# Where three sets of transposes are made in a two-layer training step: backward weights, feed-forward inputs and normalised queries

## The chip, the cores and the metric

The kernel runs on one core of a Trainium2 chip. The core has a matrix engine (TensorE, PE in the profile, with PEld for its weight loads), a vector engine (VectorE, DVE), an activation engine (ScalarE, ACT), a general engine (GpSimd, POOL) and a queueing engine (SyncE, SP), which here issues nearly all DMAs. Each engine works through its own instructions in their order; semaphores hold an instruction until what it needs is there. Sixteen DMA engines move the data. The metric is the device time of one execution in microseconds; less is better.

## What is computed

Four residual blocks in a row, and all gradients. Block A is attention without softmax over 32 heads of 16; block B is a gated feed-forward. Both share their weights between their two uses. Sequence 2048, width 512, feed-forward width 1376, bf16.

```python
def _A_ref(x, wqkv, wo):
    qkv = (x @ wqkv).reshape(B, S, 3, H, Dh).transpose(2, 0, 3, 1, 4)
    q, k, v = qkv[0], qkv[1], qkv[2]
    phi = lambda t: jnp.where(t > 0, t + 1, jnp.exp(t)) + 1e-6
    pq, pk = phi(q), phi(k)
    kv = jnp.einsum("bhsd,bhse->bhde", pk, v)
    z = jnp.einsum("bhsd->bhd", pk)
    num = jnp.einsum("bhqd,bhde->bhqe", pq, kv)
    den = jnp.einsum("bhqd,bhd->bhq", pq, z)[..., None] + 1e-6
    return (num / den).transpose(0, 2, 1, 3).reshape(B, S, D) @ wo

def _B_ref(x, w_gate, w_up, w_down):
    g = jnp.einsum("bsd,df->bsf", x, w_gate)
    u = jnp.einsum("bsd,df->bsf", x, w_up)
    return jnp.einsum("bsf,fd->bsd", _sigmoid(g) * u, w_down)

x = x + _A_ref(_layernorm(x), wqkv, wo)
x = x + _B_ref(_layernorm(x), w_gate, w_up, w_down)
x = x + _A_ref(_layernorm(x), wqkv, wo)
x = x + _B_ref(_layernorm(x), w_gate, w_up, w_down)
_out, _vjp = jax.vjp(_f, x, wqkv, wo, w_gate, w_up, w_down)
```

The outputs are the result, the gradient of x and the five weight gradients.

## The kernel before

The sequence is cut into 16 tiles of 128 rows (`st` 0 to 15). The blocks are numbered 0 to 3: 0 and 2 are attention, 1 and 3 feed-forward. In time the kernel runs these stages:

- `kq_fwd(0)`: keys, queries and the per-head products of block 0.
- `ab_fwd(0, 1)`, the *lower pass*, about 70 to 204 us: one loop over the tiles does the rest of block 0's attention and all of block 1.
- `kq_fwd(2)` and `ab_fwd(2, 3)`, the *upper pass*, about 261 to 396 us, the same for blocks 2 and 3.
- `b_bwd_p1(3)`, `a_bwd_p1(2)`, `b_bwd_p1(1)`, `a_bwd_p1(0)`: the backward stages. The products for the weight gradients (object `W`) are put between their steps and run alone for some stretches.

Order: within `manual_schedule(engines=EM)` PE, ACT, DVE and POOL take their instructions in the order in which the program writes them. SP's order is made by a planner; `tc.issue_after(ins)` holds the DMAs written in its block behind `ins` on SP's queue.

One step `st` of the two forward passes works on three tiles at once. For most steps (2 to 14, those in `HH_DMA`) the program writes:

1. POOL: a small fill of `hh_t` (L982) and `A.prod(st + 3)`, the product of queries and key sums (L840).
2. PE: `gu` for the first third of the feed-forward width (L922: four matmuls each for gate and up), with ACT's two sigmoids (L924, L926), DVE's product `hh_t` (L929) and POOL's `ssd_t` (L930).
3. `attn_y(st + 2)`: four matmuls from the transposed queries `pqnT` (L884), DVE's add (L892) and the statistics for the layer norm (DVE; POOL L452 to L455, the last making `ln_nmr`).
4. `front1(st + 3)`, `front2(st + 3)`: on DVE the row sums of `prod` (L846), their reciprocals and the normalised queries `pqnstage` (L863). After each odd tile the pair is stored to HBM (L867).
5. `finish` of an earlier tile: eleven matmuls with `wd` (L956) and DVE's add (L958). Step 3 has none.
6. the second and third `gu`; between them `ln.stage_T(st + 1)`: PE transposes the normalised input of the next tile in four blocks into PSUM (L374, `ln_tp<-ident,hstage`), and ACT copies it to the SBUF tile `hT` (L383).
7. `ln.apply(st + 2)` on ACT: the normalised input of the tile after that, `hstage` (L460).
8. `front3(st + 3)`: PE transposes `pqnstage` in four blocks (L374), ACT copies it to `pqnT`.
9. SP: `dma_T`, the DMA transpose of `hh_t` (L949), then the stores of `ssd_t` (L1051), `hh_t` to `sv_hdd` (L1052) and to `sv_hdl` (L1054), and then what `side[st]` holds, behind the last store.

The backward pass of the feed-forward needs the three weights transposed: `wdT`, `wuT`, `wgT`. In the lower pass `wT_units` makes them once: nine units, each a DMA transpose of up to 512x512 from the weight in HBM to a staging tile `wt_st` (L404, L406, L420) and a store to HBM scratch (L409, L412, L421), two of them ahead of the pass and one behind every second step. `b_weight_loads` (L198) then loads the scratch copies with plain DMAs, twice: behind steps 2, 5 and 8 of the upper pass for `b_bwd_p1(3)`, and before `b_bwd_p1(1)`. The last block of the width has 96 rows, and each matmul on it (L1250) uses 96.

In `b_bwd_p1`, `transposes` (L1198) transposes thirds of `dd` on PE, and ACT copies them to `ddT`; in the last third the full blocks (L1209) and the 96-row block (L1211) are copied apart.

## Time and profile before

| | us |
|---|---|
| median of 3 timed runs | 1138.35 (1138.16 to 1139.49) |
| the profiled execution | 1136.78 |
| its span, first to last instruction | 1135.1 |
| granted TensorE clock, mean | 0.998 of full |

Largest groups of PE, from the list of costliest groups (busy time over the whole span; the matmuls' times overlap, so that a group's time in the queue is read from one start to the next):

| line | what | instructions | busy us |
|---|---|---|---|
| L1509 | weight gradients from `p_set`, `p_a` | 2032 | 210.1 |
| L922 | gate and up | 750 | 177.4 |
| L1250 | `dh_ps` in the feed-forward's backward pass | 687 | 164.8 |
| L956 | feed-forward's last product | 340 | 80.6 |
| L374 | `ln_tp`, transposed inputs | 128 | 12.6 |
| L374 | `t_ps` and `ln_tp`, transposed queries | 120 | 11.7 |

The DMA queue that SP issues on moved 280.03 MB and was busy for 88.8% of sixteen engines' span. In a timeline the columns are start, duration (us), engine, line, operation, tiles, shapes and count; square brackets hold the engine's idle time before it and what ended it. In a table by stretch they are the stretch, its length, busy time of PE, PEld, DVE, ACT and POOL with counts, the granted clock, the DMA engines' busy share (packets overlap, so it can exceed 1) and GB/s.

### The profile page before, as it was taken

The numbers are of one execution on the slowest core, as the hardware profiler recorded it, in microseconds if no ns is written. First come the engines' busy times: TensorE is split into PE (matmuls) and PEld (weight loads), VectorE is DVE, ScalarE is ACT, GpSimd is POOL, SyncE is SP. The second block draws the span as 40 slices with busy tenths as digits, with TensorE's granted clock in tenths as the row PEclk, the third lists the DMA queues.
The fourth block names the chain that finished last, engine by engine and source line by source line (L and its number), as shares of the span: only waits on it lengthen the run. The fifth ranks groups of instructions, "written<-read, shape, count | busy, mean of one in ns | idle before, by whom it ended". The sixth has DMA issues, their size and how long they took to land. (4 is left out here: it accounts for less than half of the span.)

```text
span 1135.1 us, 19895 instructions
## 1 busy us (share of the span) xinstructions
PE 1104.4 (97%) x7358; PEld 649.9 (57%) x7468; DVE 696.4 (61%) x1344; ACT 484.6 (43%) x909; POOL 293.8 (26%) x518
## 2 busy tenths in 40 slices
PE   8989999997999999999999999999999999999998
PEld 4444554444545555554446468855556745448888
DVE  6787876777667466665975850166664976851221
ACT  6666666555665633332625431234324515410000
POOL 5647776435666400000110220000000110210000
PEclk9999999999999999999999999999999999999999
DMA  8967999855899999997999897799898899979996
GB/s 268 310 197 210 283 272 273 252 145 174 228 262 282 267 265 257 317 249 191 248 281 278 218 253 239 199 280 288 249 284 257 211 278 290 222 213 299 258 209 191
DMA packets 413682, 282.36 MB, mean 249 GB/s; under 512 B 198608, under 2 KB 399504, under 8 KB 409744
## 3 DMA queue, kind: packets, MB, share of 16 engines
q1 hardware_dynamic: 412432, 280.03, 88.8%
q8 instruction: 58, 0.95, 0.3%
q10 hardware_dynamic: 1152, 1.05, 0.3%
q14 instruction: 40, 0.33, 0.1%
HBM read 125.44 MB, written 115.70 MB: 212 GB/s over the span
## 5 line engine op out<-in xcount | busy, mean ns | idle before, releaser
L1509 PE MATMUL p_ps<-p_set,p_a 128*128 128x256 bf16 (+1 forms) x2032 | 210.1, 264 | 0.1
L1509 PEld LDWEIGHTS <-p_a 128*128 128x128 bf16 x2048 | 185.9, 98 | 22.2
L1130 DVE TENSOR_TENSOR dd<-dhh_ps,ssd 128x512 bf16<-128x512 f32 x144 | 82.4, 628 | 122.7 <-PE dhh_ps L1108 118.9
L1250 PEld LDWEIGHTS <-ddT 128*128 128x128 bf16 (+1 forms) x704 | 67.6, 98 | 74.3 <-DMA ddT<-dd 1.9
L922 PEld LDWEIGHTS <-hT 128*128 128x128 bf16 x768 | 72.8, 98 | 65.3 <-issue 0.8
L930 POOL TENSOR_TENSOR ssd_t<-hh_t,oms 128x512 bf16<-128x512 bf16 (+1 forms) x96 | 100.2, 1054 | 38.2 <-ACT hT L383 16.9
L1082 POOL TENSOR_SCALAR ab<-c 128x2 f32<-128x2 f32 x64 | 12.5, 195 | 375.5 <-DVE junk L1079 358.1
L1209 ACT COPY ddT<-T_ps 128x1024 bf16<-128x1024 bf16 (+1 forms) x72 | 58.8, 819 | 114.7 <-PE T_ps L1207 62.0
L929 DVE TENSOR_TENSOR hh_t<-u_ps,ssd_t 128x512 bf16<-128x512 f32 (+1 forms) x96 | 59.3, 631 | 59.9 <-PE u_ps L922 31.3
L1074 ACT ACTIVATE t_sb<-dh_ps,rstd_all 128x512 f32<-128x512 f32 x64 | 44.0, 688 | 116.0 <-issue 61.7
L924 ACT ACTIVATE ssd_t<-g_ps 128x512 bf16<-128x512 f32 (+1 forms) x96 | 53.4, 556 | 88.8 <-PE g_ps L922 78.7
L922 PE MATMUL u_ps<-wu,hT 128*128 128x512 bf16 (+1 forms) x378 | 89.7, 356 | 0.5
L922 PE MATMUL g_ps<-wg,hT 128*128 128x512 bf16 (+1 forms) x372 | 87.7, 357 | 0.6 <-DVE hT L381 0.2
L1483 DVE TENSOR_TENSOR dw_stg<-p_ps,dw_stg 128x512 bf16<-128x512 f32 (+3 forms) x43 | 28.1, 653 | 98.1 <-PE p_ps L1509 84.2
L1250 PE MATMUL dh_ps<-wgT,ddT 128*128 128x512 bf16 (+1 forms) x343 | 83.9, 379 | 0.4
L1250 PE MATMUL dh_ps<-wuT,ddT 128*128 128x512 bf16 (+1 forms) x344 | 80.9, 379 | 1.0 <-DMA ddT<-dd 0.4
L956 PE MATMUL y_ps<-wd,hhT 128*128 128x512 bf16 (+1 forms) x340 | 80.6, 379 | 1.2 <-DVE x L958 0.6
L1493 PE MATMUL p_ps<-p_a,p_set 128*128 128x512 bf16 (+1 forms) x342 | 80.1, 379 | 0.6
L1108 PE MATMUL dhh_ps<-wdT,gTb 128*128 128x512 bf16 (+1 forms) x323 | 72.5, 356 | 0.6
L956 PEld LDWEIGHTS <-hhT 128*128 128x128 bf16 (+1 forms) x352 | 34.3, 98 | 41.1 <-issue 0.7
L926 ACT ACTIVATE oms<-g_ps 128x512 bf16<-128x512 f32 (+1 forms) x96 | 52.7, 549 | 3.3 <-POOL ssd_t L930 2.4
L1493 PEld LDWEIGHTS <-p_set 128*128 128x128 bf16 (+1 forms) x352 | 33.5, 100 | 34.9
(227 smaller groups left out, 1817.8 us busy)
## 6 DMA issues: line engine op xcount, KB each, us to landing
p_set<-sv_hdd SPq DMA_DIRECT2D x30, 1024.0 KB, 6.1
sv_ssd<-ssd_t SPq DMA_DIRECT2D x32, 688.0 KB, 4.2
ssd<-sv_ssd SPq DMA_DIRECT2D x24, 688.0 KB, 4.9
sv_hdd<-dd SPq DMA_DIRECT2D x24, 512.0 KB, 4.4
sv_hdd<-hh_t SPq DMA_DIRECT2D x32, 320.0 KB, 4.3
p_a<-sv_h SPq DMA_DIRECT2D x16, 512.0 KB, 6.0
p_set<-sv_dqk SPq DMA_DIRECT2D x8, 1024.0 KB, 7.3
h_ld<-sv_h SPq DMA_DIRECT2D x24, 256.0 KB, 4.6
```

Of the source, the lines that this page charges most:

```text
L922: nc.tensor.matmul(ps[:, 0:w], lhsT=hT[:, kc, :], rhs=w_sb[:, kc, c0:c0 + w], start=(kc == 0), stop=(kc == NDC - 1))
L924: nc.scalar.activation(ssd_t[:, 0, c0:c0 + w], g_ps[:, 0:w], ACT.Sigmoid)
L926: nc.scalar.activation(oms[:, 0:w], g_ps[:, 0:w], ACT.Sigmoid, scale=-1.0)
L929: nc.vector.tensor_tensor(hh_t[:, c0:c0 + w], u_ps[:, 0:w], ssd_t[:, 0, c0:c0 + w], ALU.mult)
L930: nc.gpsimd.tensor_tensor(ssd_t[:, 1, c0:c0 + w], hh_t[:, c0:c0 + w], oms[:, 0:w], ALU.mult)
L956: nc.tensor.matmul(y_ps[:], lhsT=T["hhT"][0:r, fc, :], rhs=k.wd[0:r, fc, :], start=(fc == 0), stop=(fc == NFC - 1))
L1108: k.nc.tensor.matmul(ps[:, 0:w], lhsT=gT[:, jc, :], rhs=k.wdT[:, jc, c0:c0 + w], start=(jc == 0), stop=(jc == NDC - 1))
L1130: k.nc.vector.tensor_tensor(dd_part(dd, a, fs), ps[:, 0:w], ssd[:, a, c0:c0 + w], ALU.mult)
L1209: nc.scalar.copy(out[:, :, 0:nfull, :], tps[:, :, 0:nfull, :])
L1250: nc.tensor.matmul(T["dh"][:], lhsT=T["ddT"][0:r, dd_block(a, fc), :], rhs=(k.wuT, k.wgT)[a][0:r, fc, :], start=(i == 0), stop=(i == 2 * N ...
L1493: nc.tensor.matmul(ps[0:r, :], lhsT=set_t[:, st, c * P:c * P + r], rhs=self.ops[j["l"], "g"][:, st, :], start=(st == 0), stop=(st == NST - 1))
L1509: nc.tensor.matmul(ps[:, icl * w:(icl + 1) * w], lhsT=self.ops[j["l"], "h"][:, st, ic * P:(ic + 1) * P], rhs=set_t[:, st, 0:w], start=(st ...
```

## The change

1. The scratch copy of the weights and `wT_units` go. `b_weight_loads` transposes each weight from HBM straight into its SBUF tile, at both places of use, in nine units (three for each weight; the third unit of `wuT` and of `wgT` has two DMAs). In the upper pass two units follow each of steps 0 to 3 and one follows step 4. The last block now takes the last 128 columns, of which the first 32 repeat the block before; a fill on POOL sets those 32 rows to zero after the transpose, and the matmuls use all 128 rows. Accordingly `transposes` in the backward pass takes the last 128 columns of `dd`, with one ACT copy for a third.
2. The feed-forward's inputs of tiles 4 to 15, in both passes, are transposed by a DMA from `hstage` to `hT`, issued after `ln.apply(st + 2)`; tiles 0 to 3 stay on PE.
3. In the lower pass the normalised queries of tiles 6 to 15 are transposed by a DMA for each pair, issued when the odd tile is written. For this the product, `front1` and `front2` run one tile further ahead: step 2 does tiles 5 and 6, and each later step tile `st + 4`. In the upper pass queries stay on PE.

```diff
-            with tc.tile_pool(name="wt_stage", bufs=2, reuse_waits="tile") as wt_stage:
-                piece, flush = wT_units(k, wt_stage, B_w_gate, B_w_up, B_w_down)
-                piece()
-                piece()
-                A.tail()
-                ab_fwd(k, A, lns[1], {**{st: piece for st in range(0, 14, 2)}, NST - 2: flush}, nxt=lns[2])
+            A.tail()
+            ab_fwd(k, A, lns[1], {}, nxt=lns[2])
...
             def b_weight_loads():
-                def wd():
-                    k.wdT = wb.tile([P, NDC, F], BF16, name="wdT", tag="w_c")
-                    nc.sync.dma_start(out=k.wdT[:], in_=k.wT["wdT"].rearrange("(c p) f -> p c f", p=P))
-
-                def wx(nm, tag):
-                    t = wb.tile([P, NFC, D], BF16, name=nm, tag=tag)
-                    setattr(k, nm, t)
-                    nc.sync.dma_start(out=t[:, 0:NFC - 1, :],
-                                      in_=k.wT[nm][0:(NFC - 1) * P, :].rearrange("(c p) j -> p c j", p=P))
-                    nc.sync.dma_start(out=t[0:FLAST, NFC - 1, :], in_=k.wT[nm][(NFC - 1) * P:F, :])
-                return wd, lambda: wx("wuT", "w_a"), lambda: wx("wgT", "w_b")
+                tiles = {}
+
+                def by_cols(f0, w):
+                    def load():
+                        if f0 == 0:
+                            tiles["wdT"] = k.wdT = wb.tile([P, NDC, F], BF16, name="wdT", tag="w_c")
+                        return nc.sync.dma_start(out=tiles["wdT"][:, :, f0:f0 + w], in_=B_w_down[f0:f0 + w, :],
+                                                 transpose=True)
+                    return load
+
+                def by_rows(src, nm, tag, c0, n):
+                    def load():
+                        if c0 == 0:
+                            tiles[nm] = wb.tile([P, NFC, D], BF16, name=nm, tag=tag)
+                            setattr(k, nm, tiles[nm])
+                        t = tiles[nm]
+                        ins = nc.sync.dma_start(out=t[:, c0:c0 + n, :], in_=src[:, c0 * P:(c0 + n) * P], transpose=True)
+                        if c0 + n == NFC - 1:
+                            ins = nc.sync.dma_start(out=t[:, NFC - 1, :], in_=src[:, F - P:F], transpose=True)
+                            nc.gpsimd.memset(t[0:P - FLAST, NFC - 1, :], 0.0)
+                        return ins
+                    return load
+                parts = [(0, 4), (4, 3), (7, 3)]
+                return ([by_cols(f0, w) for f0, w in FSL],
+                        [by_rows(B_w_up, "wuT", "w_a", *p) for p in parts],
+                        [by_rows(B_w_gate, "wgT", "w_b", *p) for p in parts])
...
+            pieces = sum(b_weight_loads(), [])
+
+            def some():
+                for _ in range(2):
+                    if pieces:
+                        pieces.pop(0)()
             A.tail()
-            ab_fwd(k, A, lns[3], dict(zip((2, 5, 8), b_weight_loads())), out_cb=out_cb, last_cb=last_cb)
+            ab_fwd(k, A, lns[3], {st: some for st in range(5)}, out_cb=out_cb, last_cb=last_cb)
...
         def load_b_weights():
             wd, wu, wg = b_weight_loads()
-            wd()
-            wu()
+            for ld in wd + wu:
+                ld()
             with tc.issue_after(k.hold):
-                wg()
+                for ld in wg:
+                    ld()
...
-def wT_units(k, stage, B_w_gate, B_w_up, B_w_down):
...
+    def dma_T(self, st):
+        if st >= NST:
+            return
+        self.hTs[st] = hT = self.k.lnres["hT"].tile([P, NDC, P], BF16, name="hT")
+        self.k.nc.sync.dma_start(out=hT[:], in_=self.hs.pop(st), transpose=True)
...
+PQ_PE = {0: 5, 2: NST}
 FP = NFC * P
 HH_DMA = {1: range(2, NST - 1), 3: range(2, NST - 1)}
+HT_DMA = range(4, NST)
...
         if st % 2 == 1:
+            if st > PQ_PE[A.l]:
+                pqT = A.wide.tile([P, 2 * NDC, P], BF16, name="pqT")
+                nc.sync.dma_start(out=pqT[:], in_=cur["pqn"][:].rearrange("p n d -> p (n d)"), transpose=True)
+                for i in range(2):
+                    F_[st - 1 + i]["T"] = pqT[:, i * NDC:(i + 1) * NDC, :]
             nc.sync.dma_start(out=dram_batch(sva["pqn"], st // 2, 2), in_=cur["pqn"][:])
 
     def front3(st, bank="ln", evac="scalar"):
-        if st >= NST:
+        if st > PQ_PE[A.l] or st >= NST:
             return
...
-                A.prod(st + FLAG)
+                ahead = range(st + FLAG + (st > 2), st + FLAG + 2) if l == 1 else [st + FLAG]
+                for sa in ahead:
+                    A.prod(sa)
                 gu(T, hT, 0)
                 A.attn_y(st + YLAG)
-                A.front1(st + FLAG)
-                A.front2(st + FLAG)
+                for sa in ahead:
+                    A.front1(sa)
+                    A.front2(sa)
...
                 gu(T, hT, 1)
-                ln.stage_T(st + 1, "scalar")
+                if st + 1 not in HT_DMA:
+                    ln.stage_T(st + 1, "scalar")
                 gu(T, hT, 2)
...
                 ln.apply(st + YLAG)
+                if st + YLAG in HT_DMA:
+                    ln.dma_T(st + YLAG)
...
         def transposes(T, fs):
...
-            nfull = len([fc for fc in fcs if fc_rows(fc) == P])
+            n, w = len(fcs), FSL[fs][1]
...
-                for i, fc in enumerate(fcs):
-                    r = fc_rows(fc)
-                    nc.tensor.transpose(tps[0:r, a, i, :], src[:, i * P:i * P + r], k.ident[:])
+                for i in range(n):
+                    e = min((i + 1) * P, w)
+                    nc.tensor.transpose(tps[:, a, i, :], src[:, e - P:e], k.ident[:])
...
-            nc.scalar.copy(out[:, :, 0:nfull, :], tps[:, :, 0:nfull, :])
-            if nfull < len(fcs):
-                nc.scalar.copy(out[0:FLAST, :, nfull, :], tps[0:FLAST, :, nfull, :])
+            nc.scalar.copy(out, tps[:, :, 0:n, :])
...
-                r = fc_rows(fc)
-                nc.tensor.matmul(T["dh"][:], lhsT=T["ddT"][0:r, dd_block(a, fc), :], rhs=(k.wuT, k.wgT)[a][0:r, fc, :],
+                nc.tensor.matmul(T["dh"][:], lhsT=T["ddT"][:, dd_block(a, fc), :], rhs=(k.wuT, k.wgT)[a][:, fc, :],
```

## The prediction

> **What bounds the kernel now.** I read the page's first two parts, then the busy time by stretch, then the timelines of all engines in the two feed-forward passes (about 70 to 204 us lower, 261 to 396 us upper).

> ```profile
> span 1135.1 us, 19895 instructions
> PE 1104.4 (97%) x7358; PEld 649.9 (57%) x7468; DVE 696.4 (61%) x1344; ACT 484.6 (43%) x909; POOL 293.8 (26%) x518
> ...
> 112.00:196.00 84.00, 83.52 (x460) 42.64 (x468) 61.72 (x120) 54.60 (x102) 62.62 (x107) 1.00 1.02 275
> 287.00:395.00 108.00, 105.75 (x591) 54.24 (x601) 66.99 (x125) 68.68 (x132) 68.01 (x96) 1.00 0.94 265
> ```

> The matmul column (83.52 of 84, 105.75 of 108) says that PE sets the end of both passes and never waits long; the last two columns say that the DMA engines are as full (1.02 and 0.94, packets overlapping). So what leaves PE's queue is worth its own time, and whatever keeps PE waiting costs its full length.

> **What is taken off PE.** These lines are PE in step 6 of the lower pass.

> ```profile
> 126.14 0.39 PE L374 MATMUL ln_tp<-ident,hstage 128*128 128x128 bf16 x4
> 126.36 0.76 PE L922 MATMUL g_ps<-wg,hT 128*128 128x352 bf16 x4
> ...
> 129.50 0.81 PE L884 MATMUL y_ps<-M_sb,pqnT 128*128 128x512 bf16 x3
> ```

> From one start to the next, a group of four transposes occupies 0.22 us of the queue (its 0.39 us overlaps what follows). Twelve input tiles in two passes: 24 x 0.22 = 5.3 us. Query tiles 6 to 15: 10 x 0.22 = 2.2. With query tile 6 goes a wait of PE for DVE, 0.67 us before line 374 at 102.54. Gain 8.2 us. The copies out of PSUM go with them (0.58 us each on ACT, 54.60 of 84 us busy): nothing. In the backward passes a tile's two copies L1209 (577 ns) and L1211 (374 ns) become one of 128x768, about 795 ns between the 577 and the 1012 ns of 128x1024; its weights load at 98 instead of 122 ns, its matmuls stay at 379 to 381. ACT is idle most of that stage: nothing; uncovered, ACT's part would give 32 x 0.16 = 5 us back.

> **The transposed inputs** of tile st+2 are sent at the end of step st and read a step later, 8.33 us (119.44 to 127.78). Transposes of hh_t, three times as large, land in 4.3 us: nothing. They stand ahead of hh_t's own on SP, which has a step to land as well. If the queue ran more than 4 us late, each microsecond beyond would be PE's.

> **The scratch copy of the weights** leaves the lower pass: nine units of transposes, 1.4 to 3.6 us each on SP, and their stores. Nothing on PE waited for them: nothing. Hidden with them are the new transposes of the same pass.

> **The query pairs.** A pair can only be sent when its odd tile is normalised. In step 6 that is 125.08 + 0.69 = 125.77, and one step ahead of need leaves until 129.50: 3.73 us, less the 0.44 by which the step shortens, 3.29. The nearest transfer of a pair's size (256 KB) is pkT:

> ```profile
> DMA to landing us min/median/max: 3.1/3.4/4.2
> ```

> With 0.37 us from the product to SP's issue (sv_pqn at 126.14) a pair is 0.5 us late. Pair 6/7 falls after a step without a finish: ready at 102.48, read at 104.50, which itself moves 1.12 us forward (0.67 + 0.45), so 2.9 us late. Together 2.9 + 4 x 0.5 = 4.9; between 2.0 (2.5 to landing, the shortest of dq_ld; the others in time) and 8.8 (4.2). DVE does two tiles' fronts in step 2, 1.98 us more ahead of hh_t; its u bank came free at 96.1 and PE wanted it at 96.83: 1.2 us late (0 to 2).

> [...]

> **The weights of the upper pass.** Three plain loads at steps 2, 5 and 8 become eleven transposes behind steps 0 to 4, two units a step. The rate comes from a stretch with only transposes in flight and one of plain transfers:

> ```profile
> DMA packets 1824, 0.47 MB, mean 212 GB/s; under 512 B 1824, under 2 KB 1824, under 8 KB 1824
> ...
> DMA packets 253, 0.78 MB, mean 389 GB/s; under 512 B 18, under 2 KB 130, under 8 KB 253
> ```

> 4.23 MB take 19.9 instead of 10.9 us of the DMA engines, unseen by PE unless something waits. Something does: behind the last piece of wuT (step 2) and of wgT (step 4) stands a zero fill on POOL that writes into the landed tile. It is written at the step's end, so it comes ahead of the next step's POOL work, and must wait until that transpose has landed. Queued behind it: the step's product (line 840), for which DVE's row sums (846) wait, then pqnstage, then PE's query transposes; in this pass these stay on PE.

> ```profile
> 289.05 0.12 POOL L982 MEMSET hh_t<- 128x32 bf16 x1
> 289.14 1.15 POOL L840 TENSOR_TENSOR prod<-pq_all,zb 128x512 bf16<-128x512 bf16 x1
> ...
> 306.09 0.12 POOL L982 MEMSET hh_t<- 128x32 bf16 x1 [2.03 <-DMA sv_hdd<-hh_t]
> ...
> 291.89 0.65 DVE L846 TENSOR_REDUCE den<-prod 128x32 f32<-128x512 bf16 x1
> ...
> 293.18 0.69 DVE L863 TENSOR_TENSOR pqnstage<-pq_all,rden_all 128x512 bf16<-128x512 bf16 x1
> ...
> 293.93 0.40 PE L374 MATMUL t_ps<-ident,pqnstage 128*128 128x128 bf16 x4 [0.48 <-DVE pqnstage L863]
> ...
> 310.61 0.39 PE L374 MATMUL t_ps<-ident,pqnstage 128*128 128x128 bf16 x4
> ...
> 290.93 1.12 SPq L1054 DMA_DIRECT2D sv_hdl<-hh_t  x1
> 292.09 1.16 SPq L201 DMA_DIRECT2D wdT<-wdT_d  x1
> ...
> 306.83 1.23 SPq L1054 DMA_DIRECT2D sv_hdl<-hh_t  x1
> ```

> The reader sees a fill already holding POOL for a DMA at 306.09, PE already waiting on this chain at 293.93, and the weights' place on SP: right behind sv_hdl.

> First fill. sv_hdl is out at 292.05; the input transpose put ahead of it takes 1.25 on SP (pkT's issue, 1254 ns); two pieces at 1.4 each (shortest of line 420) and the last is issued at 296.1. From issue to landing I take 4.0, the median of the old weight staging's DMAs: 300.1. From POOL's release to pqnstage: 1.24 (289.05 to 290.29) and 1.98 (291.89 to 293.87), so 303.3 instead of 293.9: 9.4 us. Bounds: without the input's 1.25 and with 3.1 to landing, 7.3; with 2.6 an issue (median of line 404) and 5.1, 12.9.

> Second fill. sv_hdl out at 308.06, 1.25, one piece 1.4, last issued at 310.7, landed 314.7, pqnstage 317.9 instead of 310.6: 7.3 us (5.2 to 9.6).

> Both 16.7 (12.5 to 22.5). A gain is excluded: the fills are new, and the DMAs are issued later than POOL arrives (289.05, and 304.06 for the second). What is late next is the chain to ln_nmr behind the product; ACT's apply has PE's next two products of matmuls as cover: nothing more.

> [...]

> **The weights of the lower backward pass.** wdT's load at 589.52 (0.40 us on SP) becomes three transposes, about 5 us on SP, past pk_ld, dq_ld and hT_ld. dq_ld (the second at 592.90, 6.1 to landing, first read at 604.6) had 5.6 us to spare: 0.5 us (0 to 2). wuT and wgT land, and their fills hold POOL, where PE works through saved weight gradients from 672 to 728 (28.00 of 28): nothing; without that cover up to 8 us. p_set, issued behind wuT, is fetched two jobs ahead.

> **Sum.** -8.2 + 4.9 + 1.2 + 16.7 + 0.5 = +15.1 us. The profiled execution took 1136.8 (span 1135.1), giving 1151.9; the median of the runs is 1.6 above it, giving 1153.5. I take 1153.

> **Rivals.** (a) Forecast, 80%: the fills hold POOL. Own range 1145 (all low ends, +6.3) to 1162 (short of all high ends, +27.1).
> (b) The fills don't hold PE, 13%: POOL's place in the order isn't where the code writes them, or their transposes land before POOL comes. All else as summed: 1138.4 - 1.6 = 1136.8, not slower. It decides where POOL is free by about 290.7 and 307.4 (3.2 us ahead of PE's transposes); with the issues after 292.05 that takes another order, which speaks against it. For it: SP's order isn't written by hand.
> (c) The DMA engines become the upper pass's bound, 7%: the inputs add 1.57 MB at 212 GB/s, 7.4 us, the weights 9.0, to 0.94 x 108 = 101.5; 118 us. Stretches reach a share of 1.09, which covers it in 108 us; at 1.02 it takes 116, and the inputs come late by some 8 us: 1161 with the fills. Against it: while PE is held, the engines catch up.

> **Chances.** Within 0.2% is what the timing of this kernel can't tell from no change (1136.1 to 1140.6). Of (a) nearly all is slower, of (b) about half faster, a third same. Faster 0.10, same 0.09, slower 0.81. Range 1136 to 1161: (a) and (c) but their upper end, and half of (b).

> **What would show it.** Right: two new memsets on POOL with waits of about 10 us for wuT and wgT near 290 and 312 us, PE idle of 9 and 7 us before line-374 transposes of pqnstage there, small waits of PE for pqT at every second step of the lower pass, and 34 transpose groups gone. Wrong: PE busy through steps 2 to 5 of the upper pass, or idle before the feed-forward's first matmul with hT as releaser.

## The result and the profile after

The changed kernel takes 1166.17 us (median of 5 runs, 1165.59 to 1170.94); beside it, on the same chip, the kernel before took 1138.35 (1137.74 to 1139.49). The ratio is 1.0254 [1.0237, 1.0271]: slower by 2.5%. The forecast was 1153 in a range of 1136 to 1161: right in sign and in the place of the loss, but 13 us too small and outside its range. The profiled execution has a span of 1164.4 us, 29.3 more than before.

The page's head of the changed kernel (busy time, and the granted clock in 40 slices):

```profile
span 1164.4 us, 19715 instructions
...
PE 1108.8 (95%) x7332; PEld 643.0 (55%) x7332; DVE 699.3 (60%) x1344; ACT 464.0 (40%) x843; POOL 289.5 (25%) x522
...
PEclk9999999999879999999999999999999999999999
```

PE's share falls from 97 to 95%, and two slices of the clock row dip, which they did not before. Both dips lie in the upper pass. Busy time by stretch, the same two stretches as before, says the same:

```profile
112.00:196.00 84.00, 80.89 (x397) 38.17 (x396) 62.84 (x119) 45.12 (x83) 60.92 (x108) 1.00 0.93 239
287.00:395.00 108.00, 86.01 (x437) 41.91 (x436) 60.32 (x112) 48.38 (x95) 54.48 (x84) 0.89 0.79 205
```

In the lower pass PE is busy 80.89 of 84 us (83.52 before), with fewer instructions, and the DMA engines' share has fallen from 1.02 to 0.93. In the upper pass PE is busy 86.01 of 108 (105.75 before), at a mean clock of 0.89, and the DMA engines' share fell too (0.94 to 0.79): all wait for something that is in no engine's throughput.

To place the loss I took, in each trace, the start of the first gate matmul of each forward pass and of the first `dh_ps` matmul of each backward stage. The stage lengths between them, for all kernels of this study, which are explained below (us of one profiled execution; "rest" ends with the span). Executions of one kernel differ by several us in some of them (one unit a step: 1142.1 to 1149.2, the profiled one 1142.3; weights, fills late: 1139.4 to 1143.9, the profiled one 1143.9), so a single difference of 1 or 2 us between rows says little:

| kernel | start | lower pass | upper pass | `b_bwd(3)` | `a_bwd(2)` | `b_bwd(1)` | rest |
|---|---|---|---|---|---|---|---|
| before | 69.2 | 191.0 | 143.9 | 205.1 | 132.2 | 204.8 | 188.9 |
| the change | 67.4 | 194.9 | 167.0 | 205.0 | 135.6 | 205.6 | 188.9 |
| fills late | 68.6 | 195.8 | 150.5 | 205.0 | 135.5 | 206.7 | 189.0 |
| dummies 200/160 | 67.8 | 195.9 | 167.0 | 205.7 | 136.4 | 207.2 | 188.9 |
| dummies 265/165 | 67.5 | 198.8 | 168.9 | 205.4 | 134.9 | 206.6 | 189.6 |
| inputs alone | 67.9 | 202.8 | 148.4 | 205.1 | 132.2 | 206.8 | 191.1 |
| pairs alone | 68.5 | 219.8 | 141.9 | 205.1 | 132.3 | 207.1 | 189.5 |
| weights, fills late | 68.1 | 191.2 | 145.0 | 206.7 | 137.2 | 205.1 | 188.9 |
| weights and inputs | 69.0 | 189.5 | 149.1 | 205.0 | 132.7 | 206.5 | 190.4 |
| the same, one unit a step | 67.8 | 190.0 | 150.0 | 205.0 | 132.2 | 205.4 | 190.2 |
| the same, inputs in the lower pass only (**base**) | 68.5 | 188.8 | 142.4 | 205.0 | 134.0 | 208.3 | 189.4 |
| base, double front | 67.9 | 191.4 | 141.9 | 205.0 | 139.2 | 208.1 | 189.0 |
| base, fills at once | 68.3 | 189.6 | 162.5 | 208.9 | 133.2 | 207.0 | 189.5 |
| base, reload | 68.7 | 190.0 | 145.3 | 210.0 | 132.5 | 210.7 | 189.2 |
| base, reload later | 67.8 | 188.9 | 145.9 | 206.0 | 132.3 | 209.4 | 189.4 |
| one unit a step, third `hh_t` | 67.9 | 189.8 | 150.6 | 205.0 | 138.1 | 207.7 | 190.5 |
| base, third `hh_t` | 68.5 | 190.1 | 142.2 | 205.0 | 136.5 | 207.6 | 189.1 |

Of the change's 29.3 us, 23.1 are in the upper pass. The timeline of POOL there:

```profile
289.10 2.09 POOL L908 TENSOR_TENSOR ssd_t<-hh_t,oms 128x512 bf16<-128x512 bf16 x2 [2.04 <-ACT hT L396]
303.30 0.51 POOL L209 MEMSET wuT<- 32x512 bf16 x1 [12.11 <-DMA wuT<-in_B_w_up_dram]
303.76 0.11 POOL L960 MEMSET hh_t<- 128x32 bf16 x1
303.84 1.14 POOL L812 TENSOR_TENSOR prod<-pq_all,zb 128x512 bf16<-128x512 bf16 x1
...
331.27 0.51 POOL L209 MEMSET wgT<- 32x512 bf16 x1 [12.38 <-DMA wgT<-in_B_w_gate_dram]
```

These are the two fills that the forecast named, in program order ahead of the next step's product, waiting 12 us each for their transposes. PE answers, in its own timeline:

```profile
294.54 0.76 PE L900 MATMUL u_ps<-wu,hT 128*128 128x352 bf16 x4
307.30 0.61 PE L387 MATMUL t_ps<-ident,pqnstage 128*128 128x128 bf16 x4 [12.00 <-DVE pqnstage L835]
307.70 1.91 PE L900 MATMUL g_ps<-wg,hT 128*128 128x512 bf16 x4
...
335.27 0.61 PE L387 MATMUL t_ps<-ident,pqnstage 128*128 128x128 bf16 x4 [9.99 <-DVE pqnstage L835]
335.67 1.91 PE L900 MATMUL g_ps<-wg,hT 128*128 128x512 bf16 x4
```

Two things are to be seen. PE idles 12.00 and 9.99 us before the query transposes. And the four gate matmuls behind each wait take 1.91 us, where the same group takes 1.03 in a step without a wait: the granted clock is 0.5 from 300.3 to 310.6 and again from 327.6 to 341.3. From 307.30 and from 335.27 that costs half of 3.3 and of 6.0 us, 4.7 in all.

What the trace shows, summed: waits at the fills 22.0, half clock 4.7, waits for the query pairs 4.4, for the double front 2.8, for `hT` at 411.20 0.9, the lower backward stages 4.0, less the 8.2 taken off PE: +30.6. The kernel before had 3.4 us of half clock at 66.3 that this execution lacks (-1.7). That makes 28.9 of the 29.3. Stage by stage it fits less well, and two errors cancel. In the lower pass these terms give 1.7 us and the stage lost 3.9; a step with a late pair is longer than the recorded wait says (8.87 us from 117.82, against 7.89 for the step before it, with a wait of 0.70). In the upper pass they give 24.9 and the stage lost 23.1; PE's waits of 0.48 and 1.12 us for `pqnstage` in the kernel before (293.93 and 336.90) are gone there. The 8.2 is the forecast's figure; the 0.22 us for a group of transposes is borne out where nothing waits (a lower-pass step of the base below takes 8.11 us, against 8.33 before).

### The profile page after: what moved, and what is told of

The parts are those of the page before. It is cut to its first block, busy times and chain, and to the rows that moved or that the text cites. A ratio compares the mean times of both kernels' runs of the same rounds, so it can differ in the third digit from the quotient of the medians.

```text
span 1164.4 us, 19715 instructions
## 1 busy us (share of the span) xinstructions
PE 1108.8 (95%) x7332; PEld 643.0 (55%) x7332; DVE 699.3 (60%) x1344; ACT 464.0 (40%) x843; POOL 289.5 (25%) x522
## 3 DMA queue, kind: packets, MB, share of 16 engines
q10 hardware_dynamic: 1152, 1.05, 0.3%
## 4 chain that ended last, share of the span: by engine, by line
PE 74%; DMA 5%; DVE 4%; issue 3%; SPq 2%; POOL 1%; ACT 1%; POOLq 0%; DVEq 0%; ACTq 0%
PE p_ps L1490 16%; PE dh_ps L1231 12%; PE p_ps L1474 7%; PE dh_ps L1735 6%; PE dhh_ps L1092 6%; PE y_ps L934 4%; PE g_ps L900 3%; PE u_ps L900 3%; PE GT_ps L1631 2%; PE dp_ps L1603 2%; PE T_ps L1191 2%; PE dpk_ps L1770 2%; DMA pqT<-pqnstage 2%; PE y_ps L861 1%; PE t_mm L586 1%
## 5 line engine op out<-in xcount | busy, mean ns | idle before, releaser
L1193 ACT COPY ddT<-T_ps 128x1024 bf16<-128x1024 bf16 (+1 forms) x72 | 65.5, 913 | 117.0 <-PE T_ps L1191 62.5
L1231 PEld LDWEIGHTS <-ddT 128*128 128x128 bf16 x704 | 67.6, 98 | 75.6 <-DMA ddT<-dd 3.1
L900 PE MATMUL g_ps<-wg,hT 128*128 128x512 bf16 (+1 forms) x384 | 91.8, 362 | 1.3 <-DMA hT<-hstage 0.9
L907 DVE TENSOR_TENSOR hh_t<-u_ps,ssd_t 128x512 bf16<-128x512 f32 (+1 forms) x96 | 59.5, 632 | 54.0 <-PE u_ps L900 26.6
L1058 ACT ACTIVATE t_sb<-dh_ps,rstd_all 128x512 f32<-128x512 f32 x64 | 44.0, 687 | 118.0 <-issue 68.3
L1231 PE MATMUL dh_ps<-wgT,ddT 128*128 128x512 bf16 x352 | 85.1, 379 | 0.0
L1231 PE MATMUL dh_ps<-wuT,ddT 128*128 128x512 bf16 x352 | 81.3, 379 | 1.8 <-DMA ddT<-dd 1.8
L1092 PE MATMUL dhh_ps<-wdT,gTb 128*128 128x512 bf16 x336 | 74.2, 357 | 0.0
L1063 DVE SCALAR_TENSOR_TENSOR junk<-t_sb,h_ld 128x512 bf16<-128x512 f32 x48 | 36.4, 758 | 31.2 <-ACT t_sb L1058 26.8
```

Of the source, the lines that this page charges most:

```text
L900: nc.tensor.matmul(ps[:, 0:w], lhsT=hT[:, kc, :], rhs=w_sb[:, kc, c0:c0 + w], start=(kc == 0), stop=(kc == NDC - 1))
L907: nc.vector.tensor_tensor(hh_t[:, c0:c0 + w], u_ps[:, 0:w], ssd_t[:, 0, c0:c0 + w], ALU.mult)
L1092: k.nc.tensor.matmul(ps[:, 0:w], lhsT=gT[:, jc, :], rhs=k.wdT[:, jc, c0:c0 + w], start=(jc == 0), stop=(jc == NDC - 1))
L1193: nc.scalar.copy(out, tps[:, :, 0:n, :])
L1231: nc.tensor.matmul(T["dh"][:], lhsT=T["ddT"][:, dd_block(a, fc), :], rhs=(k.wuT, k.wgT)[a][:, fc, :], start=(i == 0), stop=(i == 2 * NFC - 1))
```

## The experiments

Each is compared with the kernel before on the same chip. "Late fills" means that the two fills of the upper pass stand at its last step.

### The fills and the clock

**Late fills.** The changed kernel, fills moved.

```diff
-                            nc.gpsimd.memset(t[0:P - FLAST, NFC - 1, :], 0.0)
+                            k.fills.append(lambda: nc.gpsimd.memset(t[0:P - FLAST, NFC - 1, :], 0.0))
+                            if not k.fills_late:
+                                k.fills.pop(0)()
...
                 if i == 0:
+                    while k.fills:
+                        k.fills.pop(0)()
+                    k.fills_late = False
...
```

> The changed kernel, with the two zero fills of the upper pass written in its last step instead of behind steps 2 and 4; every DMA stays where it was. Theory (POOL, held by the fills, holds PE): the two waits of PE of 12.0 and 10.0 us are gone, and with them the stretches at half clock behind them (some 4.6 us), so 1166.2 - 26.6 = 1139.6; up to 1143 if inputs come late now that PE gives the DMA engines no pause. Rival (the transposed loads themselves are too much for the DMA engines in steps 2 to 5): the wait moves to hT or hhT and the time stays above 1150.

Measured 1152.27 us, ratio 1.0125 [1.0111, 1.0139]: 13.9 us less than the change (12.8 when each is taken against the kernel before beside it), not the 22 to 27 that the trace puts at the fills. PE's waits in the upper pass of this kernel:

```profile
307.78 0.40 PE L393 MATMUL t_ps<-ident,pqnstage 128*128 128x128 bf16 x4 [1.03 <-DVE pqnstage L841]
318.54 0.59 PE L393 MATMUL t_ps<-ident,pqnstage 128*128 128x128 bf16 x4 [2.38 <-DVE pqnstage L841]
319.98 1.89 PE L906 MATMUL g_ps<-wg,hT 128*128 128x512 bf16 x4 [0.85 <-DMA hT<-hstage]
340.29 0.40 PE L393 MATMUL t_ps<-ident,pqnstage 128*128 128x128 bf16 x4 [1.46 <-DVE pqnstage L841]
```

The long waits are gone and short ones, absent in the change, stand in their place, with a half-clock stretch of 6.8 us at 318.6. The fills were the largest cost, but something else was late beneath them.

**Fills alone.** The later base kernel (below: one weight unit a step, late fills, inputs by DMA in the lower pass alone, queries on PE), in whose upper pass PE waits 3.5 us in all (4.4 in the kernel before), with the fills put back right behind their transposes.

```diff
-                            k.fills.append(lambda: nc.gpsimd.memset(t[0:P - FLAST, NFC - 1, :], 0.0))
-                            if not k.fills_late:
-                                k.fills.pop(0)()
+                            nc.gpsimd.memset(t[0:P - FLAST, NFC - 1, :], 0.0)
...
```

> As the kernel with one unit a step and inputs by DMA in the lower pass alone (1139.0 us), but with the two zero fills of the upper pass where the change puts them, right behind the last transpose of wuT (step 5) and of wgT (step 8). Nothing else of the upper pass is late here. Theory (a fill costs its wait and the half clock behind it, and in the changed kernel part of this was given back because inputs and queries would have been late there anyway): two waits of PE for pqnstage of 7 to 9 us, each with a half-clock stretch, 18 to 22 us in all, 1157 to 1161 us. Rival (a fill's net price is what moving both away returned in the changed kernel, 13.9 us, the rest being caught up elsewhere): 1153 us.

Measured 1160.87 us, ratio 1.0184 [1.0144, 1.0224], against 1139.01 and 1.0016 for the base. Its upper pass is 162.5 us long instead of 142.4. PE:

```profile
324.81 0.61 PE L386 MATMUL t_ps<-ident,pqnstage 128*128 128x128 bf16 x4 [8.02 <-DVE pqnstage L834]
325.21 1.91 PE L899 MATMUL g_ps<-wg,hT 128*128 128x512 bf16 x4
...
358.88 0.61 PE L386 MATMUL t_ps<-ident,pqnstage 128*128 128x128 bf16 x4 [6.13 <-DVE pqnstage L834]
359.28 1.91 PE L899 MATMUL g_ps<-wg,hT 128*128 128x512 bf16 x4
```

Waits of 14.2 us and half clock until 330.5 and 364.6 (5.7 us each, half of both lost: 5.7) make 19.9; the stage lost 20.1, as the theory had it. So here a fill's price is its wait and the half clock behind it, in full. In the changed kernel, where 13.9 us came back when both fills were moved, part of it bought time for DMAs that were late anyway.

**Dummies.** Is the half clock the answer to idling? Dummy matmuls on the identity keep PE at work where it waits, in the changed kernel:

```diff
+            if l == 3 and st in (3, 5):
+                warm_ps = ps_tile(k, "ln", [P, P], F32, "warm_ps")
+                for i in range(200 if st == 3 else 160):
+                    nc.tensor.matmul(warm_ps[:], lhsT=k.ident[:], rhs=k.ident[:], start=True, stop=True)
             if st > 0:
                 A.front3(st + FLAG, "t" if st in by_dma else "ln")
```

> The changed kernel with 200 and 160 products of the identity with itself ahead of the query transposes of steps 3 and 5 of the upper pass; nothing reads them. At 56 ns each they fill 11.1 and 8.9 us of the two waits of 12.0 and 10.0 us. Theory (the waits also cost a stretch at half clock after them, 3.3 us in the first and 6.0 us in the second, that is 1.7 and 3.0 us): the granted clock stays at 1.00, the waits for POOL stay as long, and the time is 4.6 us less, 1161.6. Rival (the slow stretch is covered by what the other engines still have to do after the hold): the clock stays up and the time stays 1166.

Measured 1169.49 us, ratio 1.0276 [1.0262, 1.0291]. The 200 dummies ended 3.27 us before `pqnstage` was there, and a half-clock stretch of 6.8 us began in that gap; the 160 left 0.21 us, and none followed. With 265 and 165:

> The changed kernel with 265 and 165 dummy identity matmuls into an unused PSUM tile ahead of the query transposes at steps 3 and 5 of the upper pass, where PE waits for the fills: PE now works through both waits, and no step waits longer. Theory (the half clock behind each wait is the answer to PE's idling): the clock stays at 1.0 through steps 3 to 6, 4.6 us less than the change, about 1161.5 us. Rival (the half clock has another cause): stretches at 0.5 behind both places, 1166 us.

Measured 1172.43 us, ratio 1.0283 [1.0261, 1.0304]. PE's timeline:

```profile
298.65 14.96 PE L1032 MATMUL warm_ps<-ident 128*128 128x128 bf16 x265
313.44 0.39 PE L387 MATMUL t_ps<-ident,pqnstage 128*128 128x128 bf16 x4
313.67 1.03 PE L900 MATMUL g_ps<-wg,hT 128*128 128x512 bf16 x4
...
341.45 0.40 PE L387 MATMUL t_ps<-ident,pqnstage 128*128 128x128 bf16 x4 [2.41 <-DVE pqnstage L835]
341.68 1.03 PE L900 MATMUL g_ps<-wg,hT 128*128 128x512 bf16 x4
342.64 1.84 PE L900 MATMUL u_ps<-wu,hT 128*128 128x512 bf16 x4
```

Now the first place has no idle time and full speed behind it (1.03), and the second has 2.41 us of idle and the half clock again (1.84). In four places the clock followed PE's idling (half speed behind gaps of 3.27 and 2.41 us, full speed behind 0.21 and none): that it is the cause is shown. The time that was expected back did not come: the two waits themselves had become longer, 14.8 and 11.8 us instead of 12.0 and 10.0, and the lower pass was 3.9 us longer than the change's. In both kernels with dummies `hhT` ahead of the first wait landed 5.3 to 5.4 us after its issue instead of 3.7; why was not settled.

### The two added transposes alone

**Inputs alone**: the kernel before with part 2's inputs. **Pairs alone**: the kernel before with part 3. The scratch copy of the weights stays in the lower pass in both.

```diff
+HT_DMA = range(4, NST)
...
-                ln.stage_T(st + 1, "scalar")
+                if st + 1 not in HT_DMA:
+                    ln.stage_T(st + 1, "scalar")
...
+                if st + YLAG in HT_DMA:
+                    ln.dma_T(st + YLAG)
...
```

> The kernel before with the feed-forward inputs of tiles 4 to 15 transposed by DMA in both passes, nothing else changed. Theory (they have a step to land, and PE loses 24 groups of transposes of 0.22 us): 1138.4 - 5.3 = 1133.1. Rival (the DMA engines are full; with the scratch copy of the weights still in the lower pass the inputs land late): waits of PE for hT and 1138 or more.

```diff
+PQ_PE = {0: 5, 2: NST}
...
+                ahead = range(st + FLAG + (st > 2), st + FLAG + 2) if l == 1 else [st + FLAG]
...
+                pqT = A.wide.tile([P, 2 * NDC, P], BF16, name="pqT")
+                nc.sync.dma_start(out=pqT[:], in_=cur["pqn"][:].rearrange("p n d -> p (n d)"), transpose=True)
...
```

> The kernel before with the queries of tiles 6 to 15 of the lower pass transposed by DMA in pairs and the fronts one tile further ahead, nothing else changed. Theory (2.9 us of PE gained; a pair is ready only 3.3 us before it is read and DVE's double step holds a u bank, 4.4 and 2.8 us as seen in the changed kernel): 1138.4 + 4.3 = 1142.7. Rival (the waits for pairs come from the new input transposes beside them on SP's queue): without these the pairs are in time and it is 1138.4 - 2.9 + 2.8 = 1138.3 or less.

Measured 1156.49 us, 1.0161 [1.0146, 1.0176], for the inputs; 1165.33, 1.0242 [1.0228, 1.0256], for the pairs. Both theories fell by some 23 us. PE in the lower pass, first with the inputs, then with the pairs:

```profile
144.94 1.04 PE L929 MATMUL g_ps<-wg,hT 128*128 128x512 bf16 x4 [1.31 <-DMA hT<-hstage]
...
201.30 1.89 PE L929 MATMUL g_ps<-wg,hT 128*128 128x512 bf16 x4 [5.27 <-DMA hT<-hstage]
```

```profile
111.00 1.89 PE L890 MATMUL y_ps<-M_sb,pqT 128*128 128x512 bf16 x4 [4.85 <-DMA pqT<-pqnstage]
132.92 1.89 PE L890 MATMUL y_ps<-M_sb,pqT 128*128 128x512 bf16 x4 [3.59 <-DMA pqT<-pqnstage]
```

In the change a pair costs 0.1 to 1.5 us; beside the weights' scratch copy 2.6 to 4.9, and each wait is followed by half clock (1.89 instead of 1.03). The lower pass takes 202.8 us with the inputs, 219.8 with the pairs. Without the scratch copy it takes 189.5 with the inputs (weights and inputs, below) and 194.9 with inputs and pairs (the change). So taking the copy out, which by itself moves nothing (191.2 against 191.0), is what makes the other two edits bearable. With the inputs it shows on SP's queue: from 100 to 190 us SP is issuing for 94% of the time in the kernel with the inputs alone and for 73% in weights and inputs, and the median time from `hstage` written to the issue of its transpose is 3.9 us (at most 7.5) against 2.0 (2.9).

**Double front.** The base with the lower pass's fronts one tile further ahead and no pair sent.

```diff
-                ahead = [st + FLAG]
+                ahead = range(st + FLAG + (st > 2), st + FLAG + 2) if l == 1 else [st + FLAG]
```

> As the kernel with one unit a step and inputs by DMA in the lower pass alone (1139.0 us), but in the lower pass the product and the queries' normalising run one tile further ahead, step 2 doing two tiles, as in the change; the queries are still transposed on PE and no pair goes by DMA. Theory (the double front alone delays hh_t, and with it the u bank, in steps 2 and 3): two waits of PE for hh_t, 2.8 us together, 1141.8 us or, if a half-clock stretch follows, 1143.5. Rival (the prediction's size): 1.2 us, 1140.2 us. Rival 2 (the waits belong to the pairs' DMA): none, 1139 us.

Measured 1143.06 us, ratio 1.0038 [1.0025, 1.005]. PE:

```profile
97.47 1.02 PE L905 MATMUL u_ps<-wu,hT 128*128 128x512 bf16 x4 [1.73 <-DVE hh_t L912]
104.17 1.02 PE L905 MATMUL u_ps<-wu,hT 128*128 128x512 bf16 x4 [0.81 <-DVE hh_t L912]
```

These are the change's waits at 97.46 and 104.16 (1.73 and 1.03): the double front alone makes them, as the theory had it. The lower pass is 2.6 us longer than the base's; half clock at the ends of the stage (3.7 us against 0.8) has a part in that.

### What is late in the upper pass

Four kernels of one comparison: **weights** (part 1 with late fills, nothing else), **weights and inputs**, the same with **one unit a step** behind steps 0 to 8, and the **base**, which has that and inputs by DMA in the lower pass only.

The first keeps all inputs on PE (`HT_DMA = range(NST, NST)`). One unit a step and the base's inputs:

```diff
-HT_DMA = range(4, NST)
+HT_DMA = {1: range(4, NST), 3: ()}
...
-                for _ in range(2):
-                    if pieces:
-                        pieces.pop(0)()
+                if pieces:
+                    pieces.pop(0)()
...
-            ab_fwd(k, A, lns[3], {st: some for st in range(5)}, out_cb=out_cb, last_cb=last_cb)
+            ab_fwd(k, A, lns[3], {st: some for st in range(9)}, out_cb=out_cb, last_cb=last_cb)
```

> Part 1 of the change alone: the weights are transposed straight into SBUF (two units behind a step in the upper pass), inputs and queries stay on PE, and the two zero fills of the upper pass stand at its last step. Theory (what is left of the loss without the fills is SP's queue being held by two units a step, some 4 us, so that stores and the query chain come late, with a half-clock stretch after it): lower pass as before, upper pass +4, lower backward stages +4, about 1146 us. Rival (the upper pass loses only because inputs go by DMA there too): upper pass +0 to +1, lower backward +4, about 1142 us. Rival 2 (weights direct cost nothing once the fills are away): 1138 us.

> Parts 1 and 2 with the fills at the last step; queries stay on PE. Beside the change with late fills (1152.3 us) only the query pairs of the lower pass and the products one tile further ahead are gone. Theory: the lower pass wins its 12 input groups, 2.6 us against before, where it lost 4.8 with the pairs: 7.4 us less, about 1145 us. Rival (the lower pass's waits move to the inputs, which then come late as they do when the scratch copy is there): lower pass no shorter than before, 1148 us or more.

> As the kernel with parts 1 and 2 and late fills, but the nine units of the upper pass stand one behind each of steps 0 to 8 instead of two behind each of steps 0 to 3. Theory (SP's queue is what is late): waits of PE for pqnstage and hT in the upper pass fall under 1 us in all, no half-clock stretch after step 3, upper pass 2 us shorter than before instead of 5 to 7 longer: about 1138 us. Rival (the DMA engines' share of time is the limit, whichever step the units stand behind): the waits move to steps 5 to 9 and the upper pass stays 5 us longer than before, about 1145 us.

> As the kernel with one unit a step, but the inputs go by DMA in the lower pass alone; the upper pass has them on PE. Theory: the upper pass is as long as before (weights one unit a step cost nothing there, inputs bring nothing), lower pass 2.6 us shorter, lower backward +4: about 1139 us. Rival (inputs by DMA in the upper pass are what cost there): this one is faster than the kernel with inputs in both passes by over 3 us. Rival 2 (inputs by DMA win their 2.6 us in the upper pass too): it is slower than that one by 2 to 3 us.

| kernel | us | ratio |
|---|---|---|
| weights, fills late | 1140.62 (1139.39 to 1143.94) | 1.0038 [1.0021, 1.0055] |
| weights and inputs | 1144.25 (1143.92 to 1148.74) | 1.0075 [1.0049, 1.01] |
| the same, one unit a step | 1147.91 (1142.11 to 1149.23) | 1.0077 [1.005, 1.0104] |
| base | 1139.01 (1137.62 to 1142.78) | 1.0016 [1.0005, 1.0028] |

The first came out near its rival's 1142, the second and the base as their theories (1145 and 1139). The theory that two units a step hold SP fell: spreading them left the upper pass at 150.0 us (149.1 before the spreading). Where the inputs stay on PE it takes 145.0 with two units a step and 142.4 with one, less than before's 143.9. So it is the inputs by DMA that cost there, 4 to 8 us, where the sum had a gain of 2.6. They cost it also where the weights still come by plain loads: 148.4 us with the inputs alone, against 143.9. In the lower pass they do gain: 188.8 to 190.0 us against 191.2.

What is late? PE in the upper pass with one unit a step:

```profile
335.45 0.40 PE L392 MATMUL t_ps<-ident,pqnstage 128*128 128x128 bf16 x4 [1.03 <-DVE pqnstage L840]
...
355.70 1.04 PE L905 MATMUL g_ps<-wg,hT 128*128 128x512 bf16 x3 [1.44 <-DMA hT<-hstage]
```

and POOL, in the changed kernel with late fills:

```profile
325.66 0.12 POOL L966 MEMSET hh_t<- 128x32 bf16 x1 [3.87 <-DMA sv_hdl<-hh_t]
```

POOL's small fill of `hh_t` waits for the buffer's stores, and product and queries wait behind the fill. The theory was that the stores are late because the inputs stand ahead of them on SP. The upper pass has two buffers of `hh_t`, the lower three. A **third `hh_t`**, with a buffer of `out_t` and one of `pqnT` given up:

```diff
-                     hh=wide.tile([P, FP], BF16, name="hh_t", bufs=3 if l == 1 else 2),
+                     hh=wide.tile([P, FP], BF16, name="hh_t", bufs=3),
...
```

> As the kernel with late fills, one unit a step and inputs by DMA in both passes (1147.9 us), but hh_t has three buffers in the upper pass as it has in the lower (out_t and the upper pass's pqnT give up one each for the room). Theory (inputs by DMA lose in the upper pass because they stand ahead of hh_t's stores on SP, POOL's small fill at the head of the step after next waits for the buffer, and product, pqnstage and PE's query transposes wait behind it): POOL's waits for sv_hdd and sv_hdl go, and with them PE's waits for pqnstage (4.3 us there); the waits for hT (3.7) stay or shrink; upper pass 139.5 to 144 instead of 150 us, 1135 to 1141 us. Rival (the inputs are late of themselves): PE's waits move to hT, 1146 us or more.

> As the kernel with one unit a step and inputs by DMA in the lower pass alone (1139.0 us), with the three buffers of hh_t in the upper pass. Theory: that kernel's upper pass had almost no waits for the buffer, so nothing changes: 1138.5 to 1139.5 us. Rival (giving up a buffer of out_t or pqnT costs): slower than 1140.5 us.

Measured 1150.28 us, 1.0095 [1.0064, 1.0126]; the control 1142.14, 1.0027 [1.001, 1.0044]. The rival holds: POOL's waits for the buffer are gone, but the upper pass takes 150.6 us, and PE waits elsewhere:

```profile
317.93 1.04 PE L905 MATMUL g_ps<-wg,hT 128*128 128x512 bf16 x4 [1.18 <-DMA hT<-hstage]
...
356.09 1.04 PE L905 MATMUL g_ps<-wg,hT 128*128 128x512 bf16 x3 [2.48 <-DMA hT<-hstage]
```

So freeing this buffer moved the waits and won nothing. The buffer of `out_t` given up blurs this a little: ACT now waits for its stores (2.76 us at 343.09). But ACT waits for them in the control too, and the control's upper pass takes 142.2 us, as the base's does; its own 3 us more than the base lie in other stages, and its theory of no change fell.

Where the inputs' lateness arises can be read from the transposes themselves. In the kernel with one unit a step, the twelve of the lower pass are issued 2.0 us (median; at most 2.8) after `hstage` is written, and land 2.7 us after that. The twelve of the upper pass are issued 4.0 us (at most 7.0) after it and land 3.2 us after that. So most of the difference lies ahead of the issue, on SP's queue. The worst one, which ends in the wait at 355.70 above, in ACT's and SP's timelines:

```profile
344.24 0.81 ACT L429 ACTIVATE hstage<-x,ln_nmr,rstd_all 128x512 bf16<-128x512 f32 x1 [0.16 <-POOL ln_nmr L424]
...
346.13 2.09 SPq L206 DMA_TRANSPOSE wgT<-in_B_w_gate_dram  x1
348.26 1.26 SPq L208 DMA_TRANSPOSE wgT<-in_B_w_gate_dram  x1
349.63 1.27 SPq L932 DMA_TRANSPOSE hhT<-hh_t  x1
351.00 1.00 SPq L456 DMA_DIRECT2D sv_h<-hstage  x1
352.05 1.72 SPq L471 DMA_TRANSPOSE hT<-hstage  x1
```

SP issues one DMA after the other here, and the input's turn comes 7 us late. What makes the queue late stays open: the issues of the weights' pieces vary in length (the large ones take 2.0 to 3.4 us in this pass); that the load of the DMA engines holds them was not shown. By the engines' share alone the kernels don't differ: between 318 and 356 us it is 1.07 in the base, and 1.07 and 1.03 in the two kernels with inputs.

### The lower backward stages

The base gains 3.7 us on the kernel before by the end of the upper pass (399.7 against 404.1 us, less 0.7 at its start) and loses 5.7 in the stages behind it. **Reload**: the landed weights are stored to HBM and loaded again with plain DMAs, the stores in front of `b_bwd(3)`, or (**later**) behind it.

```diff
+                    for nm in ("wdT", "wuT", "wgT"):
+                        nc.sync.dma_start(out=scratch(nm), in_=getattr(k, nm)[:])
...
-            wd, wu, wg = b_weight_loads()
...
+            def load(nm, tag, n, w):
+                t = wb.tile([P, n, w], BF16, name=nm, tag=tag)
+                setattr(k, nm, t)
+                nc.sync.dma_start(out=t[:], in_=scratch(nm))
...
```

> As the kernel with one unit a step and inputs by DMA in the lower pass alone (1139.0 us), but the lower backward pass loads the three weights with plain DMAs again: behind the upper pass the landed tiles, zero rows included, are stored to HBM, and loaded from there. Theory (direct transposes in the lower backward pass cost some 3 to 5 us, by SP's queue, late loads and p_set): the stages behind the upper backward feed-forward pass take as long as before, 1134 to 1135 us, faster than the kernel before by 0.2 to 0.3%. Rival (those stages lose time for another reason, since they also lost 2 us where their code was untouched): 1137 to 1139 us.

> As the kernel that stores the landed weights and reloads them with plain DMAs, but the three stores stand behind the upper backward feed-forward pass, where the DMA engines had a share of 0.69 to 0.85 before, instead of in front of it (there they landed 8 to 11 us after issue and PE idled 3.25 us for dd). Theory (direct transposes cost the lower backward pass 3 to 5 us, and the loss of the earlier stores was their place alone): upper backward pass as long as before, later stages as before: 1134 us, 0.3% faster than before. Rival (the later stages lose 2 to 6 us whichever way the weights come): 1137 to 1140 us. Rival 2 (the stores hold the attention weights' loads that reuse their buffers): PE waits for woT or wqkvT, 1140 us or more.

Measured 1147.20 us, 1.007 [1.0053, 1.0086], and 1141.50, 1.0026 [1.0014, 1.0037]; the theory fell both times. Plain loads do hold `a_bwd(2)` at 132.2 to 132.5 us in every kernel that has them; with direct transposes it took 132.2 to 139.2. But `b_bwd(1)` lost 0.3 to 5.9 us in every kernel, 2.0 and 2.3 in the two whose backward code is that of before. In the kernel with the later stores PE waits there:

```profile
837.53 2.55 PE L1248 MATMUL dh_ps<-wuT,ddT 128*128 128x512 bf16 x11 [1.24 <-DMA ddT<-dd]
854.73 1.47 PE L1248 MATMUL dh_ps<-wuT,ddT 128*128 128x512 bf16 x6 [1.77 <-DMA ddT<-dd]
```

Before, the wait at this place was 0.44; in the base there are two, of 1.23 and 1.53. What sets them is open; from 800 to 865 us the DMA share is 0.99 before and 1.04 to 1.05 in the base and with inputs alone. No kernel here is faster than the one before; the base comes nearest.

## Why the forecast was right in sign and short in size

The forecast's sum was +15.1 us and the account of the trace is +28.9. The missing 13.8 are 5.3 at the fills, 4.7 of half clock, 3.5 in the lower backward stages, 1.6 at the double front and 0.9 for the inputs, less 0.5 at the pairs and the 1.7 that this execution saved at 66 us. The forecast's own high ends came to +27.1, or 1165.5 us; its range ended at 1161, short of them.

**The fills hold POOL (forecast, 80%): right in mechanism, the term was mis-sized.** 16.7 us were put at the two fills, with bounds of 12.5 and 22.5. The waits came to 22.0, near the upper bound. SP's timeline of the change shows where:

```profile
294.62 1.03 SPq L1038 DMA_DIRECT2D sv_hdl<-hh_t  x1
295.69 4.16 SPq L206 DMA_TRANSPOSE wuT<-in_B_w_up_dram  x2
299.89 1.26 SPq L208 DMA_TRANSPOSE wuT<-in_B_w_up_dram  x1
...
324.66 1.24 SPq L1038 DMA_DIRECT2D sv_hdl<-hh_t  x1
325.95 2.08 SPq L206 DMA_TRANSPOSE wgT<-in_B_w_gate_dram  x1
328.07 1.26 SPq L208 DMA_TRANSPOSE wgT<-in_B_w_gate_dram  x1
```

- A large piece takes 2.1 us on SP (two in 4.16), not 1.4: 1.4 us at the first fill, 0.7 at the second. The 1.4 was the shortest of line 420, which transposes `w_down`; the old staging's transposes of `w_up` itself (L404) took 2.1 us at the least.
- From the fill's start to `pqnstage` used by PE it is 4.0 us (303.30 to 307.30), not 3.2: the fill's own 0.51 was left out, though it is an instruction on the same engine; the rest is time between the engines. That is 0.8 for each.
- The pieces start late against PE. At the first fill they start 0.4 us behind the end of PE's last matmul (295.69 against 295.30), where the sum had them 0.6 ahead: 1.0 us. At the second they start 0.7 behind it (325.95 against 325.28), where the sum had them 1.3 ahead: 2.0 us. SP was still busy with the units of the steps before (two of them took 4.81 us from 313.78).
- Landing was shorter than the 4.0 taken (3.4 and 3.2 from the last issue to the fill), which gives back 0.6 and 0.8.

**The clock (no term): missing.** 4.7 us behind the two waits. The step that failed is "ACT's apply has PE's next two products of matmuls as cover: nothing more": the wait was priced as its own length only. The kernel before shows the rate, at 66.3 us, behind PE's waits of 1.63 and 1.23 us (granted clock 0.50 from 66.3 to 69.7), and it was not read. That idling lowers the clock, the dummies show (half speed behind gaps of 3.27 and 2.41 us, full speed behind 0.21 and none).

**Pairs (4.9 us; 2.0 to 8.8): right in mechanism, in size partly by luck.** The waits come to 4.4 in the changed kernel's lower pass, but as 1.49, 0.70, 0.66, 0.12 and 1.46 us for the five pairs, where the sum had 2.9 for the first and 0.5 for each other one. And the term was taken from a trace with the scratch copy in it, beside which the pairs cost far more (below).

**Double front (1.2 us; 0 to 2): mis-sized.** 2.8 us, 2.5 by itself. The sum followed one bank at one place; DVE's lateness meets PE twice, in the first third's up product of step 3 (97.46) and in that of step 4 (104.16).

**Transposed inputs (a step to land: nothing): right in the lower pass, wrong in the upper.** The upper pass loses 4 to 8 us by them once the fills are away. The change's own trace shows only 0.9 of it; that the fills' waits let the DMAs catch up there is the likely reason (the engines' share is 0.59 from 295 to 308 us and 0.50 from 325 to 336). The step that failed is "a step to land": it took the time from issue to landing against the time of a step. The forecast named the condition (a queue over 4 us late) but put it at nothing without reading how late the queue of the upper pass would be. In the kernel with one unit a step it is late by 4.0 us (median) to 7.0, with 3.2 to land behind it. POOL's wait for the buffer of `hh_t`, which stood among the forecast's lines (2.03 us for `sv_hdd`), does not explain it: the third `hh_t` took such waits away and the loss stayed.

**Scratch copy (nothing on PE): right by itself** (191.2 us against 191.0). That its going carries the other two edits was said in one clause ("Hidden with them are the new transposes of the same pass"), without a price; with the copy in place the inputs cost 13 us of the lower pass more (202.8 against 189.5) and the pairs 25 (219.8 against 194.9).

**Lower backward (0.5 us; 0 to 2): mis-sized.** 4.0 us in this execution: `hT_ld`, `pkT`, `p_set` and `ddT` late. The change's trace:

```profile
646.99 1.04 PE L1770 MATMUL dpk_ps<-Nv,hT_ld 128*128 128x512 bf16 x4 [0.99 <-DMA hT_ld<-sv_hT]
...
716.10 7.16 PE L1490 MATMUL p_ps<-p_set,p_a 128*128 128x256 bf16 x64 [0.71 <-DMA p_set<-sv_hdd]
...
866.32 2.55 PE L1231 MATMUL dh_ps<-wuT,ddT 128*128 128x512 bf16 x11 [1.55 <-DMA ddT<-dd]
```

It was `hT_ld` that came late and not `dq_ld`, and "p_set is fetched two jobs ahead" did not cover it. Part of the 4 us appears also where the code was not touched, so that not all of it is the weights'.

**Rivals.** (b) is out: both fills waited. (c), the DMA engines as the upper pass's bound, was given 7%. Something like it lies beneath the stalls of (a): with late fills the upper pass still takes 150.5 us, 6.6 more than before, near the 8 of (c). But that the engines set it is not shown; the transposes are late before they are issued, and the engines' share is the same where nothing is lost (from 318 to 356 us 1.07 in the base, 1.07 and 1.03 in the two kernels with inputs).

## What to carry to other kernels

Where an instruction waits for a DMA on an engine that works in order, price the whole chain behind it. For the change's first fill that was the issues ahead of the DMA at the durations of a busy queue (2.1 us for a large piece), the landing (3.4), the fill's own time and every step up to PE (4.0 together), and the half clock after PE had idled 12.00 us (half of 3.3). Whether a transposing DMA hid was decided here by its wait on the queue ahead of the issue (a median of 2.0 us in the lower pass, where the inputs gained, and of 4.0 in the upper, where they lost) as well as by its landing (2.7 and 3.2), so read both for the stage where it will stand. Edits that share a queue didn't add here (with the scratch copy in place the pairs cost the lower pass 25 us more): try each alone and each taken out, since one edit's stall can hide another's lateness (13.9 us came back at the fills, of the 22 to 27 that the trace put there).

## What the hardware showed

PE's granted clock fell to 0.5 for 3.41 us in the kernel before (from 66.3), for 10.24 and 13.65 us in the change (from 300.3 and 327.6) and for 6.8 us with late fills (from 318.6): one, three, four and two times 3.41. Where the program ends, the last stretch is cut short (2.40 us before, 2.58 in the change). It fell after idle times far shorter than the fills' waits: 2.41 and 3.27 us in the kernels with dummies. The length of one idle did not decide it. Behind 3.27 us in the kernel with 200 dummies four gate matmuls took 1.91 us (311.05) instead of 1.03; behind 3.25 us in the kernel with the reload (418.06) four matmuls of 352 columns took 0.76, as in steps without a wait. In the kernel before the clock fell at 66.3 us, in the second of two waits of 1.63 and 1.23 us; the changed kernel kept its full clock through three waits of 1.73, 1.03 and 1.49 us, at 97.46, 104.16 and 106.68 us.
